# Five edits to the data movement of a convolution-and-token-mixing kernel: x in DRAM by chunks, merged halo copies, channel weights and chunk 2 at other times

## Chip, cores, metric

One core of a Trainium2 chip (trn2). The metric is the device time of one execution in microseconds (us); medians are over executions. The profile is one execution on that core, taken by the hardware profiler.

## The reference, cut to what matters

```python
# x: (8, 4224, 192), weight: (8, 7); w_tok_r, w_tok_i: (4224, 4224); w_theta, w_ch: (192, 192)
w = softmax(weight)                                   # 7 taps for each of 8 heads
x = causal_conv(x, w)                                 # along the sequence, by head
theta = x @ w_theta
zr, zi = x * cos(theta), x * sin(theta)
y = einsum('ts,bsd->btd', w_tok_r, zr) + einsum('ts,bsd->btd', w_tok_i, zi)
u = x + y
out = u + maximum(u @ w_ch, 0.0)
```

The two products over the sequence (4224 by 4224, 1536 columns) are nearly all of the arithmetic. The kernel makes them in seven real products in place of eight, by sums of the weights and of zr and zi.

## The kernel before: what the change and the argument touch

The sequence is cut into 33 chunks of 128 tokens, each of four runs of 32 tokens from the four quarters of the sequence. A chunk is loaded, convolved, rotated (`theta`, `product`, `sums`) and kept in SBUF as the moving operand. Eleven chunks are held at a time. A *step* goes over the chunks held, for two tiles of 128 output tokens; its weights are loaded by GpSimd's queue (`load_w`: 4 loads of w_tok_r, 4 of w_tok_i), transposed by VectorE in 32-blocks (`turn`) and combined (`wsum`). In the *ramp*, the first 110 us, the first eleven chunks come in while the first steps already run.

```python
xs = dram.tile([S, N], F16, name="xs")       # the convolved x, kept in DRAM for the residual
...
class Chunk:
    def __init__(self, k, before=None):
        self.xw = wk.tile([2 * WR, 2, B, D], F16, name="xw", tag="big", bufs=6)
        for a in range(NQ):                           # the four quarters
            h, lo = a // 2, (a % 2) * WR
            t0 = token(k, a)
            hist = self.xw[lo : lo + HALO, h, :, :]
            if before is not None:                    # 16 tokens of the chunk before
                nc.sync.dma_start(
                    out=hist, in_=before.xw[lo + Q : lo + Q + HALO, h, :, :]
                )
            ...
            nc.gpsimd.dma_start(                      # 96 KB of x
                out=self.xw[lo : lo + n, h, :, :],
                in_=x[:, t0 : t0 + n, :].rearrange("b s d -> s b d"),
            )
    def conv(self, j):
        ...
        if j == 1:
            for a in range(NQ):                       # four stores of 96 KB
                t0 = token(self.k, a)
                nc.sync.dma_start(out=xs[t0 : t0 + Q, :], in_=self.x[a * Q : (a + 1) * Q, :])
...
st = wpool.tile([P, 2, NQ, NW * Q], F16, name="st", tag="st", bufs=2)   # in load_w: two buffers
...
steps[0].load_rows()
for m in (1, 2):
    steps[0].load_w(m)      # weights r, then i, of step 0
load_chunk(2)
for m in (1, 2):
    steps[1].load_w(m)      # each needs the buffer that step 0's transposes free
for i in range(NW + 2):     # the ramp: one round a chunk
    ...
    if i + 3 < NW:
        load_chunk(i + 3)
    ...
dve(nc.vector.memset(wch[:, 1:3, :], 0.0))            # at the end of the ramp
for rows, i, part_w in channel_pieces(moe_w_ch):
    nc.gpsimd.dma_start(out=wch[rows, i, :], in_=part_w)
```

The weights' staging tile `st` has two buffers: the r half of step 1 can only be loaded when the r half of step 0 has been transposed, and the i half when the i half has. And GpSimd issues in the order of the program: in the trace of before, chunk 3's load goes out at 20.96 us, behind step 1's weights.

## Time and profile before

| | before |
|---|---|
| time, first three runs | 1445.77, 1449.16, 1449.5 us |
| profiled span | 1446.4 us |
| TensorE busy | 1416.3 us (98%) |
| TensorE busy in the first 110 us | 92.2 us |
| TensorE idle from 110 to 1370 us | 2.9 us |
| granted TensorE clock, mean | 0.998 |

Read it from the last rows up: the middle of the kernel is full, so the time can only change at the two ends, and the ramp is the larger. The lines behind this are in the prediction below.

### The profile page before, as it was taken

What the parts mean: (1) busy time and instruction counts of PE and PEld (TensorE: products, weight loads), DVE (VectorE), ACT (ScalarE), POOL (GpSimd) and SP (SyncE); (2) the same over time, 40 slices, a digit from 0 to 9 for tenths busy, and PEclk for the clock granted to TensorE, in tenths of its full rate; (3) what the DMA queues carried; (4) which work ended last, traced back from release to release, by engine and by line L of the source; (5) the groups of instructions that cost most, each with busy time, mean ns of one, the idle gap of its engine ahead of it and who ended that gap; (6) DMA issues with size and microseconds to landing.
All of it is one profiled execution on the core that took longest, in us unless ns stands there. A gap on an engine that the chain in (4) does not pass through costs nothing.

```text
span 1446.4 us, 23748 instructions
## 1 busy us (share of the span) xinstructions
PE 1416.3 (98%) x9809; PEld 887.9 (61%) x9809; DVE 979.2 (68%) x1051; ACT 315.5 (22%) x379; POOL 435.1 (30%) x655
## 2 busy tenths in 40 slices
PE   7899999999999999999999999999999999999997
PEld 5556666666666666666666666666666666666665
DVE  6893555545548777866666657877777667767686
ACT  5861101111134254000000004435210110010133
POOL 7431211111233232432433342233323123213120
PEclk9999999999999999999999999999999999999999
DMA  9986756465699998998899989999999999998893
GB/s 173 227 178 145 146 103 149 90 149 97 137 231 219 214 250 217 228 254 183 213 256 213 242 143 245 228 188 234 279 216 206 209 204 221 204 203 194 166 222 125
DMA packets 272029, 281.99 MB, mean 195 GB/s; under 512 B 106672, under 2 KB 240176, under 8 KB 271920
## 3 DMA queue, kind: packets, MB, share of 16 engines
q0 software_dynamic: 162464, 92.15, 48.4%
q1 hardware_dynamic: 71824, 178.88, 35.1%
q10 hardware_dynamic: 37632, 9.44, 4.1%
q8 instruction: 77, 1.26, 0.3%
q14 instruction: 32, 0.26, 0.1%
HBM read 245.49 MB, written 108.13 MB: 244 GB/s over the span
## 4 chain that ended last, share of the span: by engine, by line
PE 89%; DVE 4%; DMA 3%; POOL 2%; ACT 1%; issue 1%; SPq 0%; DVEq 0%; ACTq 0%; POOLq 0%
PE y L443 82%; PE v L141 5%; PE pc L210 1%; PE tp L165 1%; POOL st L323 1%; DMA xw<-in_x_dram 1%; DVE z L257 1%; DVE wt L336 1%; DVE pv L408 1%; ACT z L246 1%; DVE z L251 0%; DVE pv L476 0%; DVE wt L348 0%; POOL xw L197 0%; DMA xs<-z 0%
## 5 line engine op out<-in xcount | busy, mean ns | idle before, releaser
L443 PE MATMUL y<-z,wt 128*128 128x384 f16 x7656 | 1283.6, 326 | 10.6 <-DVE pv L408 7.5
L443 PEld LDWEIGHTS <-wt 128*128 128x128 f16 x7656 | 740.8, 98 | 488.6 <-issue 10.6
L408 DVE TENSOR_TENSOR pv<-y,pv 128x768 f32<-128x768 f32 x324 | 308.9, 954 | 323.6 <-PE y L443 282.8
L336 DVE STREAM_TRANSPOSE wt<-st 128x1408 f16<-128x1408 f16 (+7 forms) x224 | 327.8, 1465 | 48.5 <-PE y L443 39.0
L323 POOL DMA_DIRECT2D st<-in_moe_w_tok_r_dram x232 | 132.5, 578 | 466.1 <-DVE wt L336 461.0
L323 POOL DMA_DIRECT2D st<-in_moe_w_tok_i_dram x232 | 132.7, 578 | 404.4 <-DVE wt L336 388.9
L348 DVE TENSOR_TENSOR wt<-wt 128x1408 f16<-128x1408 f16 (+7 forms) x216 | 176.7, 818 | 40.8 <-PE y L443 38.4
L151 ACT ACTIVATE z<-pc 128x768 f16<-128x768 f32 x65 | 53.2, 819 | 387.2 <-PE pc L210 386.9
L151 ACT ACTIVATE ub<-pv 128x768 f16<-128x768 f32 x63 | 50.2, 835 | 333.0 <-DVE pv L408 310.4
L406 ACT ACTIVATE pv<-y 128x768 f32<-128x768 f32 x66 | 54.0, 819 | 282.0 <-PE y L443 282.0
L141 PEld LDWEIGHTS <-uT 128*128 128x128 f16 x1056 | 91.0, 98 | 25.8 <-issue 7.9
L386 POOL TENSOR_TENSOR pv<-pv,xr 128x1536 f32<-128x1536 f32 x24 | 74.5, 3105 | 68.6 <-DVE pv L476 22.1
L197 POOL DMA_DIRECT2D xw<-in_x_dram x132 | 76.4, 585 | 31.0 <-DMA xw<-xw 8.7
L476 DVE SCALAR_TENSOR_TENSOR pv<-v,pv 128x768 f32<-128x768 f32 x66 | 62.9, 954 | 27.5 <-PE v L141 27.1
L257 DVE TENSOR_TENSOR z<-z 128x768 f16<-128x768 f16 x132 | 73.4, 556 | 3.6
L151 ACT ACTIVATE uT<-tp 128x1536 f16<-128x1536 f16 (+1 forms) x48 | 58.2, 1215 | 74.4 <-PE tp L165 74.4
L246 ACT ACTIVATE z<-v,half_pi 128x768 f16<-128x768 f32 x66 | 59.8, 907 | 41.2 <-PE v L141 40.8
L251 DVE TENSOR_TENSOR z<-z 128x1536 f16<-128x1536 f16 x66 | 60.0, 947 | 7.5 <-ACT z L246 7.5
L141 PE MATMUL v<-wth,uT 128*128 128x192 f16 x528 | 55.0, 248 | 4.4 <-ACT z L246 3.0
L141 PE MATMUL v<-wch,uT 128*128 128x192 f16 x528 | 54.2, 246 | 2.1 <-DVE pv L476 1.2
L246 ACT ACTIVATE z<-v 128x768 f16<-128x768 f32 x66 | 53.4, 809 | 0.0
L210 PE MATMUL pc<-xw,bands 96*64 96x192 f16 x528 | 35.8, 258 | 2.6 <-ACT bands L625 1.1
(44 smaller groups left out, 142.4 us busy)
## 6 DMA issues: line engine op xcount, KB each, us to landing
part<-pv SPq DMA_DIRECT2D x79, 768.0 KB, 4.3
pv<-part SPq DMA_DIRECT2D x79, 768.0 KB, 6.1
out_dram<-pv SPq DMA_DIRECT2D x66, 384.0 KB, 4.3
st<-in_moe_w_tok_r_dram POOLq DMA_DIRECT2D x136, 176.0 KB, 5.5
st<-in_moe_w_tok_i_dram POOLq DMA_DIRECT2D x136, 176.0 KB, 5.1
xs<-z SPq DMA_DIRECT2D x132, 96.0 KB, 4.5
xw<-in_x_dram POOLq DMA_DIRECT2D x121, 96.0 KB, 6.1
xr<-xs SPq DMA_DIRECT2D x24, 384.0 KB, 3.7
```

The source lines that it names most:

```text
L141: pe(nc.tensor.matmul(v[:, k, b * D : (b + 1) * D], lhsT=tT[:, 3 * k + b + i, :], rhs=w[:, 2 * b + i, :], start=(i == 0), stop=(i == 1),))
L151: act(nc.scalar.activation(out=out, in_=in_, func=AT.Copy))
L197: nc.gpsimd.dma_start(out=self.xw[lo : lo + n, h, :, :], in_=x[:, t0 : t0 + n, :].rearrange("b s d -> s b d"),)
L246: act(nc.scalar.activation(**args))
L257: dve(nc.vector.tensor_tensor(out=z[:, o, :], in0=z[:, a, :], in1=z[:, b, :], op=ALU.subtract))
L323: pool(nc.gpsimd.dma_start(out=st[a * Q : (a + 1) * Q, 0:nb, :, 0:n] .rearrange("i r bt s -> i (r bt) s"), in_=w[self.tbs[0] * P : (self.t ...
L336: dve(nc.vector.transpose(self.w[name][:, 0 : self.n, :, :], self.st[int(name[1])][:, int(name[0]) - 1, :, 0 : self.n * Q] .rearrange("p b ...
L348: dve(nc.vector.tensor_tensor(out=self.w[name][:, 0 : self.n, :, :], in0=self.w[a][:, 0 : self.n, :, :], in1=self.w[b][:, 0 : self.n, :, : ...
L386: ins = pool(nc.gpsimd.tensor_tensor(out=self.pv[i], in0=self.pv[i], in1=self.xr[i], op=ALU.add))
L408: dve(nc.vector.tensor_tensor(out=o, in0=yv, in1=o, op=ALU.add))
L443: pe(nc.tensor.matmul(y[cn][:, q, 0:BH], lhsT=self.w[wn][:, c, :, :].rearrange("p bt i -> p (bt i)"), rhs=chunks[k].z[:, zn, q * BH : (q + ...
L476: dve(nc.vector.scalar_tensor_tensor(out=ub, in0=channel_mix(self.uT[i][:, 6 * g : 6 * g + 6, :], wch), scalar=0.0, in1=ub, op0=ALU.max, o ...
```

## The change

The intent: fewer DMA issues on SyncE in the ramp (one store of x a chunk in place of four; halo rows of both halves in one copy, so two copies a chunk in place of four), the load of the channel weights taken off the end of the ramp into a quiet step, and x of chunk 2 on GpSimd's queue ahead of the weights of step 0.

```diff
-    xs = dram.tile([S, N], F16, name="xs")
+    xs = dram.tile([NK, P, N], F16, name="xs")
 ...                                                   # Chunk.__init__
+            for lo in (0, WR) if before is not None else ():
+                nc.sync.dma_start(
+                    out=self.xw[lo : lo + HALO, :, :, :],
+                    in_=before.xw[lo + Q : lo + Q + HALO, :, :, :],
+                )
 ...                                                   # the copies of one half each are gone
-                    nc.sync.dma_start(
-                        out=hist, in_=before.xw[lo + Q : lo + Q + HALO, h, :, :]
-                    )
+                    pass
 ...                                                   # conv
-                for a in range(NQ):
-                    t0 = token(self.k, a)
-                    nc.sync.dma_start(
-                        out=xs[t0 : t0 + Q, :], in_=self.x[a * Q : (a + 1) * Q, :]
-                    )
+                nc.sync.dma_start(out=xs[self.k, :, :], in_=self.x)
 ...                                                   # load_x: x read back, four loads for one
-            nc.sync.dma_start(
-                out=self.xr[i], in_=xs[self.tbs[i] * P : (self.tbs[i] + 1) * P, :]
-            )
+            for j in range(NQ):
+                a, k = divmod(NQ * self.tbs[i] + j, NK)
+                nc.sync.dma_start(
+                    out=self.xr[i][j * Q : (j + 1) * Q, :],
+                    in_=xs[k, a * Q : (a + 1) * Q, :],
+                )
 ...                                                   # step_events
+        if t == NU - 2:
+            def load_wch():
+                dve(nc.vector.memset(wch[:, 1:3, :], 0.0))
+                for rows, i, part_w in channel_pieces(moe_w_ch):
+                    pool(nc.gpsimd.dma_start(out=wch[rows, i, :], in_=part_w))
+            found.append((3, load_wch))
 ...
     steps[0].load_rows()
+    load_chunk(2)
     for m in (1, 2):
         steps[0].load_w(m)
-    load_chunk(2)
 ...
-    dve(nc.vector.memset(wch[:, 1:3, :], 0.0))
-    for rows, i, part_w in channel_pieces(moe_w_ch):
-        nc.gpsimd.dma_start(out=wch[rows, i, :], in_=part_w)
```

Cut: the accumulating stores of the last tiles (`add_ahead`), which now go by runs of rows in the new layout.

More of the change, by code (lines that the diff above doesn't have):

```diff
@@ L133, in token, with x_rows @@
         return (a * NK + k) * Q
+    def x_rows(tb):
+        found = []
+        for j in range(NQ):
+            a, k = divmod(NQ * tb + j, NK)
+            if found and found[-1][2] == a:
+                found[-1][1].append(k)
+            else:
+                found.append((j * Q, [k], a))
+        return [
+            (slice(lo, lo + len(ks) * Q), slice(ks[0], ks[-1] + 1), slice(a * Q, (a + 1) * Q))
+            for lo, ks, a in found
+        ]
     def channel_mix(tT, w):
@@ L185, in __init__ @@
                 t0 = token(k, a)
-                hist = self.xw[lo : lo + HALO, h, :, :]
                 if before is not None:
-                    nc.sync.dma_start(
-                        out=hist, in_=before.xw[lo + Q : lo + Q + HALO, h, :, :]
-                    )
+                    pass
                 elif t0 == 0:
-                    nc.vector.memset(hist, 0.0)
+                    nc.vector.memset(self.xw[lo : lo + HALO, h, :, :], 0.0)
                 else:
@@ L378, in load_x @@
             self.xr[i] = wk.tile([P, N], F16, name="xr", tag="xr", bufs=1)
-            nc.sync.dma_start(
-                out=self.xr[i], in_=xs[self.tbs[i] * P : (self.tbs[i] + 1) * P, :]
-            )
+            for j in range(NQ):
+                a, k = divmod(NQ * self.tbs[i] + j, NK)
[3 more added lines that the diff above has]
+                )
         def add_x(self, i):
@@ L393, in add_ahead @@
             tb = self.tbs[i]
-            for cols in (slice(0, HN), slice(HN, N)):
-                pool(nc.gpsimd.dma_start(
-                    out=part[which][tb, :, cols], in_=xs[tb * P : (tb + 1) * P, cols],
-                    accum_op=ALU.add,
-                ))
+            for rows, ks, a in x_rows(tb):
+                for cols in (slice(0, HN), slice(HN, N)):
+                    pool(nc.gpsimd.dma_start(
+                        out=part[which][tb, rows, cols].rearrange("(k i) n -> i k n", i=Q),
+                        in_=xs[ks, a, cols].rearrange("k i n -> i k n"), accum_op=ALU.add,
+                    ))
         def give(self, y, i, h, copies):
```

## The prediction

> **What bounds the kernel now.** I read the page first for the share of each engine, then a table of stretches to see where TensorE is not full, then the waits and the timeline of those stretches, and last the landing times of the single DMAs there.
>
> The first lines of the page:
>
> ```profile
> PE 1416.3 (98%) x9809; PEld 887.9 (61%) x9809; DVE 979.2 (68%) x1051; ACT 315.5 (22%) x379; POOL 435.1 (30%) x655
> ...
> PE   7899999999999999999999999999999999999997
> ```
>
> TensorE is full except in the first slices and the last. The table by stretches (length; then busy us of PE, PEld, DVE, ACT, POOL; granted clock, DMA share, GB/s) gives sizes:
>
> ```profile
> 30.00:40.00 10.00, 6.58 (x56) 4.28 (x55) 8.22 (x15) 7.07 (x9) 4.58 (x8) 0.94 1.30 212
> ...
> 100.00:110.00 10.00, 7.54 (x48) 4.33 (x46) 9.79 (x12) 0.63 (x1) 3.40 (x6) 1.00 0.59 78
> 110.00:400.00 290.00, 290.00 (x1786) 174.64 (x1785) 145.51 (x126) 38.31 (x48) 58.58 (x103) 1.00 0.61 128
> ...
> 1030.00:1370.00 340.00, 340.00 (x2275) 216.78 (x2274) 241.14 (x237) 37.84 (x48) 97.22 (x122) 1.00 0.95 204
> 1370.00:1447.00 77.00, 67.00 (x547) 46.14 (x544) 54.34 (x67) 25.70 (x33) 9.34 (x17) 0.99 0.67 173
> ```
>
> From 110 to 1370 us TensorE misses 2.9 us in all (0 in the two long stretches shown; 0.73, 0.73 and 1.41 in the three between them). The idle 30.1 us (1446.4 less 1416.3) lie at the two ends: about 17 us in the first 110 us (the ramp, in which the first 11 chunks of x are convolved, rotated and multiplied) and 10 us in the last 77. The start-to-start time of two large matmuls in the trace has a median of 163 ns[...]. In the ramp the idle time is less than what is lost: 33 dummy matmuls and a granted clock of 0.89 to 0.94 between 30 and 50 us are in it too. Counting the matmuls that the ramp needs by their spacing in the trace (258 large ones at 163 ns, 176 at 82 ns, 132 transposes at 56 ns, 22 convolutions of about 0.5 us, 2.5 us for the bands) gives about 77 of 110 us. So some 33 us, 2.3% of the span, is the most that any repair of the ramp alone could earn.
>
> The waits of TensorE in the ramp (total us, times, longest), and the rows of the timeline (start, duration) that the change touches:
>
> ```profile
> PE y L443 <- DVE pv L408: 5.1, 5, 2.5
> ...
> PE pc L210 <- DMA xw<-in_x_dram: 0.9, 1, 0.9
> ```
>
> ```profile
> 12.36 2.29 POOL L197 DMA_DIRECT2D xw<-in_x_dram  x4
> ...
> 16.41 2.29 POOL L323 DMA_DIRECT2D st<-in_moe_w_tok_r_dram  x4 [1.77 <-DVE wt L336]
> ...
> 20.96 4.57 POOL L197 DMA_DIRECT2D xw<-in_x_dram  x8
> ...
> 27.70 0.52 PE L210 MATMUL pc<-xw,bands 96*64 96x192 f16 x7 [0.88 <-DMA xw<-in_x_dram]
> ...
> 103.52 0.22 DVE L699 MEMSET wch<- 128x192 uint32 x1
> 103.66 0.90 DVE L408 TENSOR_TENSOR pv<-y,pv 128x768 f32<-128x768 f32 x1
> ...
> 104.61 10.57 PE L443 MATMUL y<-z,wt 128*128 128x384 f16 x64 [2.46 <-DVE pv L408]
> ```
>
> The load at 12.36 is chunk 2. The one wait of TensorE for x, at 27.70, is for chunk 3, whose fourth piece was issued at 22.67 and landed at 27.66; it was not chunk 2, whose pieces landed from 15.7 to 18.9 while its convolution ran at 20.53 in program order, after dummies.
>
> [...]
>
> **The change part by part.** *One store of x a chunk.* 132 stores become 33. One takes SyncE 0.42 us to issue (tile view of xs in the ramp), so 99 x 0.42 = 42 us of issue go, 1.3 us a chunk. VectorE later overwrites the x that the store reads, which must wait for it. But the group of those subtractions (L257) has 3.6 us of idle time in the whole run and none of it is put down to a DMA. On the path: 0.
>
> *Halo copies.* 120 become 60, at 0.54 us: 32 us of SyncE go. A copy must still wait for the last of the loads of the chunk before; only the copies ahead of the last one shrink. TensorE has no wait for a halo copy in its list. On the path: 0, perhaps 0.3 us gained through less traffic at 20 to 28 us.
>
> *x read back.* 24 loads of 384 KB become 96 of 96 KB: 72 x 0.42 = 30 us of SyncE added, and the last of four is issued 1.3 us later. GpSimd's additions waited 2.3 us in all for these loads and VectorE 1.3 us for one addition, in a stretch where TensorE lost 0.7 us. On the path: 0, at worst 1. The accumulating stores go from 18 to 20: of the nine late tiles only one spans two quarters of the sequence. GpSimd is busy 97 of 340 us there: 0.
>
> *Channel weights.* The memset sits on VectorE at 103.52, straight ahead of the addition that TensorE waits for; VectorE has no gap from 85.6 us on. It delays that addition by 103.66 - 103.52 = 0.14 us (operations overlap a little). Gain 0.14, and with it may go up to 1 us of GpSimd waiting that nobody waits for. In its new place, around 3/7 of the sixteenth step, VectorE is half idle: 0.
>
> *Chunk 2 sooner.* On GpSimd's queue its four issues, 2.29 us, go from 12.36 to 7.77, and the token weights of step 0 go back by 2.3 us. In the trace these landed at 11.7 to 13.0 and 13.2 to 14.7, and VectorE took them at 15.35 and 16.36. Moved by 2.3 us, the first half lands at up to 15.4 and the second at up to 17.0, so the transposes at 15.35 and 16.36 slip by 0.1 to 0.6 us. Their end frees the buffer for the issue at 16.41; from there GpSimd issues without a break to the load of chunk 3, which may be 0.5 us later. But that DMA queue was moving data without pause from 20 to 28 us, and chunk 2's bytes are now out of the way earlier, so its landing should move by less: -0.5 to +0.5, taken as 0. What chunk 2 itself gains is invisible, for its convolution did not wait.
>
> Sum on the path: 0.14 sure, about 0.3 from lighter traffic, 0 to 1 against it. I take a gain of 0.5 us from the page's kernel. The three plain runs (1445.77, 1449.16, 1449.5) average 1448.1; less the gain that is 1447.6, and I say 1447.8.
>
> **Rivals.** (a) The early order matters more: after 30 us ScalarE and VectorE pass the chunks on with little slack (ScalarE 9.3 to 9.9 of each 10 us from 40 to 60), so a start of chunk 3 that moves early or late shifts the whole ramp[...]. For it: the chain of waits runs through the issue at 16.41 and the landing at 27.66. Against: the chunk that moves is not the one waited for. It would make 2 to 4 us either way: 1444 to 1451. (b) The SyncE queue is the hidden brake of the ramp: between 19 and 33 us it issues almost without a pause, and a third less of it frees halo copies and stores by 1 to 2 us a chunk. For it: copies landed 4 to 6 us after issue. Against: TensorE waited for no halo copy, VectorE for no store. If true, 3 to 6 us faster, 1442 to 1445. (c) Four loads in the place of one hold up SyncE's in-order queue in the middle, and partial sums come late. For it: SyncE waited 73.7 us for GpSimd at this load. Against: there are only 24 such tiles, in a stretch where TensorE hardly waits. One late addition in four would cost 24/4 x 1.3 = 8 us: 1456.
>
> **Range and chances.** The runs of before spread over 3.7 us, more than the effect. The range takes that spread, (a) whole and the near end of (b): 1444.6 to 1450.8. Faster by 2% means under 1420; even (b) is far from it, and only the whole 33 us of the ramp would do: 0.01. Slower by 2% needs 29 us, several times (c): 0.01.
>
> **What would show it.** Right: TensorE still busy about 1416 us and idle about 30; 110 to 1370 us unchanged; the wait for chunk 3 near 27 us still there within 1 us; the wait at the end of the ramp about 0.15 us shorter with no memset ahead of it; SyncE's issues for xs, halo and x read back at 33, 60 and 96. Wrong: if the first step of full rate comes more than 2 us sooner or later than 104.6, (a) or (b) holds; if waits of large matmuls for VectorE between 520 and 1370 us grow, (c).

Its sum: 0.14 us sure, about 0.3 from lighter traffic (estimate, for which no trace is named), 0 to 1 against it, taken together as a gain of 0.5. That the middle is full rests on TensorE's 2.9 us of idle time from 110 to 1370 us; that its matmuls could not follow one another faster than every 163 ns was not shown.

## The result, and the profile after

| | before | after |
|---|---|---|
| median (range; executions) | 1448.92 (1445.77 to 1449.5; 4) | 1451.8 (1451.25 to 1452.16; 4) |
| ratio, after over before | | 1.0024, 95% interval 1.0007 to 1.0041 |
| profiled span | 1446.4 | 1449.5 |
| TensorE busy in the first 110 us | 92.2 | 88.95 |

A ratio here is the mean time of one kernel's fast runs over that of the other's of the same rounds, so it is not quite the ratio of the medians that are quoted. The change is some 3 us slower, where a gain of about 0.5 was predicted, and 1451.8 lies 1.0 us above the end of the predicted range.

First the page of the kernel after:

```profile
PE 1416.0 (98%) x9809; PEld 887.7 (61%) x9809; DVE 976.6 (67%) x1051; ACT 315.4 (22%) x379; POOL 437.7 (30%) x657
...
PE   7789999999999999999999999999999999999997
```

TensorE's work is the same (1416.0 against 1416.3 us), so the 3.1 us are idle time, and the second and third slices are at 7 and 8 where they were at 8 and 9. The stretches of the kernel after (length; busy us of PE, PEld, DVE, ACT, POOL; clock, DMA share, GB/s) say the same:

```profile
20.00:30.00 10.00, 7.55 (x60) 4.67 (x57) 8.78 (x15) 5.10 (x7) 7.80 (x14) 0.83 0.96 163
30.00:40.00 10.00, 5.95 (x58) 4.12 (x59) 6.99 (x12) 8.01 (x10) 5.89 (x11) 1.00 1.35 217
...
110.00:400.00 290.00, 290.00 (x1786) 174.66 (x1785) 147.87 (x129) 38.12 (x47) 59.25 (x105) 1.00 0.62 127
1030.00:1370.00 340.00, 340.00 (x2271) 216.53 (x2270) 241.36 (x236) 37.84 (x48) 97.44 (x120) 1.00 0.98 204
```

From 110 to 1370 us TensorE is idle for 2.9 us, as before: so the four loads of x read back, the new place of the channel weights and the accumulating stores cost nothing on the path. From 20 to 30 us it executes 60 matmuls; in the kernel before the same stretch is

```profile
20.00:30.00 10.00, 8.25 (x86) 5.57 (x85) 9.56 (x14) 6.94 (x10) 7.84 (x14) 1.00 1.36 206
```

26 more, at a full clock, and with the DMA engines at 206 GB/s in place of 163. The loss begins there. The waits of TensorE in the first 115 us of the kernel after (total, times, longest):

```profile
PE y L459 <- DVE pv L424: 6.0, 6, 2.3
...
PE v L155 <- DVE uT L163: 1.9, 2, 1.8
PE pc L226 <- DMA xw<-in_x_dram: 1.7, 1, 1.7
```

The wait of the convolution for x of chunk 3 has gone from 0.9 to 1.7 us, and a wait of 1.8 us for a copy by VectorE is new. Where do they come from? The timeline of the kernel after (start, duration, engine, operation; in brackets the idle time before it and what ended it):

```profile
7.77 2.32 POOL L213 DMA_DIRECT2D xw<-in_x_dram  x4
...
13.31 2.42 SPq L198 DMA_DIRECT2D xw<-xw  x4
13.86 1.72 POOL L335 DMA_DIRECT2D st<-in_moe_w_tok_i_dram  x3 [0.92 <-DMA xw<-in_x_dram]
...
20.45 0.45 DVE L348 STREAM_TRANSPOSE wt<-st 128x256 f16<-128x256 f16 x1 [4.11 <-DMA st<-in_moe_w_tok_i_dram]
...
22.20 2.29 POOL L335 DMA_DIRECT2D st<-in_moe_w_tok_i_dram  x4 [3.60 <-DVE wt L348]
...
23.16 0.83 PE L155 MATMUL v<-wth,uT 128*128 128x192 f16 x8 [1.77 <-DVE uT L163]
...
24.48 5.70 POOL L213 DMA_DIRECT2D xw<-in_x_dram  x10
...
31.28 0.52 PE L226 MATMUL pc<-xw,bands 96*64 96x192 f16 x7 [1.70 <-DMA xw<-in_x_dram]
```

Read it as one chain, from the top:

1. Chunk 2 is issued at 7.77 (12.36 before). The i half of step 0's weights follows behind it; three of its four issues also wait 0.92 us.
2. The landing records put the four pieces of that half at 14.9, 18.0, 18.9 and 20.3 us (before: 13.2 to 14.7).
3. VectorE's transpose of it stands idle for 4.11 us and starts at 20.45 (before: 16.36). In VectorE's order the copy of chunk 1's transpose stands behind it and is late as well (22.15 against 19.71): the 1.77 us wait of TensorE at 23.16.
4. That transpose and the next (it ends at 21.91) free the staging buffer: step 1's i half goes out at 22.20 (before: 18.68), and chunk 3 behind it at 24.48 (before: 20.96).
5. Chunk 3 lands 3.6 us later (last piece 31.2 against 27.66), and TensorE waits for it.

Between steps 3 and 4 the delay shrinks from 4.10 to 3.52 us. In the kernel before, the second transpose of the i half ended at 17.80, but GpSimd came to the issue that waits for it only at 18.68:

```profile
16.36 0.44 DVE L336 STREAM_TRANSPOSE wt<-st 128x256 f16<-128x256 f16 x1
...
17.36 0.44 DVE L336 STREAM_TRANSPOSE wt<-st 128x256 f16<-128x256 f16 x1
...
18.68 2.29 POOL L323 DMA_DIRECT2D st<-in_moe_w_tok_i_dram  x4
```

In the kernel after, the issue follows the end of that transpose by 0.3 us (21.91 and 22.20). So before had about 0.6 us to spare, and only what a slip has beyond that reaches chunk 3.

From here the two traces are parallel. Against the first trace of the kernel before, the evacuation of chunk 3's convolution is 3.58 us later, VectorE's transpose at 56.4 us is 3.09 later, and everything after 107 us is 2.94 later. (The step from 3.58 to 3.09 lies where the trace of before has a window at half clock, explained below.) The 0.15 us between the last two is the memset, which no longer stands ahead of this addition:

```profile
106.54 0.95 DVE L424 TENSOR_TENSOR pv<-y,pv 128x768 f32<-128x768 f32 x1
```

### The profile page after: what moved, and what is told of

Same layout as the page of the kernel before. It is cut to its first block, busy times and chain, and to the rows that moved or that the text cites. A ratio compares the mean times of both kernels' runs of the same rounds, so it can differ in the third digit from the quotient of the medians.

```text
span 1449.5 us, 23566 instructions
## 1 busy us (share of the span) xinstructions
PE 1416.0 (98%) x9809; PEld 887.7 (61%) x9809; DVE 976.6 (67%) x1051; ACT 315.4 (22%) x379; POOL 437.7 (30%) x657
## 2 busy tenths in 40 slices
DMA packets 269707, 281.97 MB, mean 195 GB/s; under 512 B 105312, under 2 KB 238816, under 8 KB 269600
## 4 chain that ended last, share of the span: by engine, by line
PE 90%; DVE 4%; DMA 2%; ACT 2%; POOL 1%; issue 1%; DVEq 0%; SPq 0%; POOLq 0%; ACTq 0%
PE y L459 82%; PE v L155 5%; PE tp L179 1%; PE pc L226 1%; DMA xw<-in_x_dram 1%; ACT z L258 1%; DVE pv L424 1%; DVE z L263 1%; DMA xw<-xw 1%; DVE z L269 1%; ACT uT L165 1%; DVE pv L492 0%; POOL xw L213 0%; DVE wt L360 0%; DVE wt L348 0%
```

## The experiments

The question is which of the edits makes step 0's weights land so late. The expectations name theories by letters. *Theory O*: the new order alone does it; 2.3 us of issues ahead of step 0's weights. *Theory Q*: SyncE's queue does it. In the kernel after, the reads of x for the first tile stand early in SyncE's queue (at 19.02, 22.58 and 30.76 us; before, the first such read is at 82.6), and they wait there for the stores to land (7.1 us in two waits, the longest 4.0), with the halo copies behind them. *Theory B*: the *merged halo copies* or the *single store* crowd the DMA engines. *Theory D* is the late landing read above, whatever makes it; *theory C* is that executions differ only in how many windows at half clock they meet.

**How small differences were told apart.** Every kernel was timed, but the intervals of a ratio are about 0.0013 either way, some 2 us, not much less than the effect. So each kernel's trace was also laid beside the first trace of the kernel before, operation by operation, and three shifts were read: VectorE's third transpose (16.36 us before), the evacuation of chunk 3's convolution (28.25 us), and the end of the ramp (VectorE's additions after 165 us). All shifts below are against that one trace; + is later. It has a half-clock window of its own at 38.87 us: against kb_before, whose ramp has none, every figure of the last column is 1.17 larger (4.11 for after).

| kernel | median us | ratio to before, 95% interval | third transpose | chunk 3 evacuated | end of ramp |
|---|---|---|---|---|---|
| after | 1451.8 | 1.0024 (1.0007 to 1.0041) | +4.10 | +3.58 | +2.94 |
| k0_after (the same again) | 1452.5 | 1.0015 (1.0001 to 1.0029) | +3.08 | +2.77 | +3.57 |
| kb_before (before again) | 1449.59 | 1.0009 (0.9995 to 1.0023) | +0.05 | -0.25 | -1.17 |
| k1_order | 1449.17 | 1.0003 (0.9987 to 1.0019) | +1.03 | -0.50 | -1.41 |
| k3_halo | 1450.32 | 1.0 (0.9988 to 1.0013) | +0.03 | +1.61 * | +3.58 * |
| k4_layout | 1449.99 | 1.0009 (0.9997 to 1.0021) | +0.04 | +2.88 * | +4.63 * |
| k2_noorder | 1451.6 | 1.001 (0.9998 to 1.0022) | +0.44 | +2.45 * | +3.89 * |
| k6_all_minus_halo | 1450.96 | 0.9997 (0.9981 to 1.0014) | +1.92 | +2.42 * | +4.62 * |
| **k1b_order_halo** | 1451.66 | 1.0019 (1.0007 to 1.0031) | +4.27 | +3.00 | +4.71 (* 1.68 of it) |
| k14_order_halo_split | 1449.96 | 1.0004 (0.9993 to 1.0016) | +0.36 | +0.08 | +1.36 (* 1.68 of it) |
| k5_wch | 1449.94 | 0.9999 (0.9987 to 1.0011) | +0.06 | +0.25 | +0.12 |
| k10_before_c3 | 1450.21 | 1.0007 (0.9994 to 1.002) | +0.03 | -0.64 | +1.78 (* 1.68 of it) |
| k12_order_c3_wch | 1450.54 | 1.0008 (0.9996 to 1.002) | +1.10 | -0.64 | -0.75 |
| k15_after_c3 | 1449.14 | 1.0001 (0.9988 to 1.0014) | +2.47 | -0.97 | -0.67 |
| k7_held | 1456.24 | 1.0053 (1.0033 to 1.0073) | +4.27 | +3.33 | +3.62 |
| k9_held_c3 | 1453.12 | 1.0031 (1.0004 to 1.0058) | +2.90 | -0.68 | +0.56 |

(*) A window at half clock sits in these figures. What it explains of them, and what it does not, comes first.

**The windows at half clock.** In 13 of the 17 kept traces TensorE is granted half its clock in some windows of 3.41 us of the ramp. The clock records of the traces of before and after have two values, 1.0 and 0.5, and in the ramp lengths that are whole multiples of 3.413 us: 23.893 us (7 times) at full clock and 3.413 at half in the kernel before, 10.240 (3 times) and 3.413 in the kernel after. Three stretches of the first trace of the kernel before, then the last of them in kb_before, which is the same program (the number after POOL's is the clock):

```profile
32.05:35.46 3.41, 1.90 (x16) 1.05 (x14) 2.61 (x4) 3.41 (x5) 2.96 (x6) 1.00 1.25 199
35.46:38.87 3.41, 1.79 (x16) 0.81 (x15) 3.26 (x7) 1.61 (x3) 1.15 (x2) 1.00 1.30 221
38.87:42.28 3.41, 3.41 (x22) 2.12 (x21) 3.38 (x6) 2.06 (x3) 1.91 (x4) 0.50 0.64 97
```

```profile
38.87:42.28 3.41, 2.83 (x30) 2.06 (x29) 3.41 (x6) 2.89 (x5) 2.17 (x4) 1.00 0.94 135
```

A window with 1.79 us of busy TensorE (52%) was followed by one at half clock, with 22 matmuls where kb_before ran 30 in less busy time. The window before these in the first trace, from 32.05 us, was busy for 1.90 us (56%) and was followed by a full clock. Busy time alone does not decide it: windows that were 41% busy (k4_layout, at 105.37 us) and 44% (k9_held_c3, at 103.27) were followed by a full clock too. What brings the half clock was not shown. The half-clock window starts at 38.87 us in the first trace of before and at 24.32 in that of after, and kb_before, the program of before, has none in the ramp; so they are counted here as chance between executions. By the two figures of the trace such a window would cost 3.41 x 0.5 = 1.7 us where TensorE is the limit (an estimate); the shift measured across one at 105 to 112 us was 1.68 (k1b_order_halo, k3_halo, k10_before_c3). The two traces of before differ by 1.17 us at the end of the ramp; how much of the spread of that kernel, from 1445.77 to 1454.9 in all rounds, such windows make was not shown. They make single traces at the end of the ramp poor witnesses. The first two shifts are better ones. Where half-clock windows lie before 32 us, the evacuation is starred, but the clock is the smaller part of those figures. In k2_noorder, k3_halo, k4_layout and k6_all_minus_halo TensorE first waited for a DMA, in a window that it filled to 12 to 33%, and the half clock followed; it lengthened the seven matmuls before the evacuation from 0.52 to 0.82 or 0.85 us. The rest of 1.6 to 2.9 us is the wait for the DMA. Not starred are after and k7_held, whose window at 24.3 and 24.6 us is followed by a wait of TensorE for chunk 3 (1.7 and 1.5 us), so that it cost nothing there, and k14_order_halo_split, whose window from 8.86 to 19.1 us slowed matmuls (the eight of a convolution took 0.85 us at 14.01 and 17.14, 0.52 at 21.33). In k14_order_halo_split, k2_noorder and k6_all_minus_halo a full-clock window lies before that, from 5.3 to 5.5 us on, and the first store of x went out 1.1 us sooner than in the other traces (11.79 against 12.8 to 12.9).

### One part of the change at a time

**k1_order**: the kernel before, with chunk 2 moved ahead alone.

```diff
     steps[0].load_rows()
+    load_chunk(2)
     for m in (1, 2):
         steps[0].load_w(m)
-    load_chunk(2)
```

> The kernel before with nothing changed but the place of chunk 2's load on GpSimd's queue, ahead of the token weights of step 0. Theory O (order: the weights of step 0 now wait behind chunk 2 in GpSimd's one ring, so VectorE's third transpose of the ramp, at 16.36 us before and 20.45 us after, is late and everything behind it too): the third transpose at 19 to 20.5 us and the whole span 2 to 3.5 us longer than before. Theory B (burst: the one store of x and the merged halo copies crowd the DMA engines just when the second half of these weights is under way): the third transpose at no later than 17.5 us and the span within 1 us of before.

The i half landed at 15.0 to 17.3 us and the transpose slipped by 1.03 us, no more:

```profile
17.38 0.45 DVE L336 STREAM_TRANSPOSE wt<-st 128x256 f16<-128x256 f16 x1 [1.28 <-DMA st<-in_moe_w_tok_i_dram]
...
21.40 6.92 POOL L197 DMA_DIRECT2D xw<-in_x_dram  x12
```

Chunk 3 was issued 0.44 us later (21.40 against 20.96) and evacuated 0.50 sooner; the ratio is 1.0003. (Of the slip of 1.03, 0.6 was to spare.) Theory O falls: alone, the new order does nearly what the prediction said of it.

**k2_noorder**: the kernel after, with chunk 2 put back.

```diff
     steps[0].load_rows()
-    load_chunk(2)
     for m in (1, 2):
         steps[0].load_w(m)
+    load_chunk(2)
```

> The kernel after with chunk 2's load put back behind the token weights of step 0; store, halo copies and channel weights stay changed. Theory O: the third transpose back at 16.4 us within 0.5, the span at or 0.2 us below before. Theory B: the third transpose still 1 us or more late, the span 1 us or more above before. Theory Q (queue: the reads of x for one tile now sit among the first entries of SyncE's in-order queue and hold up halo copies behind them): the third transpose in time, but conv of chunks 3 to 5 late, span 1 to 3 us above before.

The transpose was at +0.44 us: without the order the late weights are gone. But chunk 3 was late by another way, the one that theory Q names: its halo copies stood in SyncE's queue behind a read of x that waited for a store, went out only at 23.09 and landed at 28.57, and TensorE waited 2.7 us for them and then 0.9 us for x. The half clock from 29.24 us came after that. The median of 1451.6 has an interval that includes 1, so the time is inconclusive.

**k3_halo** and **k4_layout**: the kernel before with the merged halo copies alone, and with the new layout of x (one store, four loads, accumulating stores by runs) alone.

```diff
+            for lo in (0, WR) if before is not None else ():        # k3_halo
+                nc.sync.dma_start(
+                    out=self.xw[lo : lo + HALO, :, :, :],
+                    in_=before.xw[lo + Q : lo + Q + HALO, :, :, :],
+                )
 ...
-                for a in range(NQ):                                 # k4_layout
-                    t0 = token(self.k, a)
-                    nc.sync.dma_start(
-                        out=xs[t0 : t0 + Q, :], in_=self.x[a * Q : (a + 1) * Q, :]
-                    )
+                nc.sync.dma_start(out=xs[self.k, :, :], in_=self.x)
```

> The kernel before with the merged halo copies alone. Theory O and Q: within 0.5 us of before. Theory B: part of the loss, 0.5 to 1.5 us above before.

> The kernel before with the layout of x in DRAM alone: one store a chunk, four loads for a tile, the accumulating copies by groups of rows. Theory O: within 0.5 us of before. Theory B: 0.5 to 1.5 us above. Theory Q: 1 to 3 us above, with the convolution of chunk 3 or 4 late although its x has landed, and SyncE seen waiting for stores of x ahead of halo copies.

Neither moved the transpose (+0.03 and +0.04), and neither interval excludes 1. So no part alone makes step 0's weights as late as in the kernel after, and two together are to be tried. But chunk 3 was late in both traces. In k4_layout a read of x waited in SyncE's queue for a store up to 23.18, and the halo copies of chunk 3 behind it, the last of which landed at 30.14; its x had landed by 27.40:

```profile
23.18 0.32 SPq L391 DMA_DIRECT2D xr<-xs  x1
23.59 2.41 SPq L202 DMA_DIRECT2D xw<-xw  x4
...
28.53 0.24 PE L224 MATMUL pc<-xw,bands 96*64 96x192 f16 x1 [1.46 <-DMA xw<-xw]
...
30.28 0.82 PE L224 MATMUL pc<-xw,bands 96*64 96x192 f16 x7 [1.50 <-DMA xw<-xw]
```

This is what the expectation gave as the sign of theory Q. In k3_halo TensorE waited 1.9 us for x of chunk 3, issued 0.8 us later than in before. These are executions of 1452.1 and 1452.35 us, above the medians of their kernels; whether the others did the same is not on record, and the ratios (1.0009 and 1.0) show no clear loss.

**k5_wch**: the channel weights moved alone.

```diff
+            found.append((3, load_wch))       # in the step t == NU - 2
 ...
-    dve(nc.vector.memset(wch[:, 1:3, :], 0.0))
```

> The kernel before with the channel weights alone in their new place. By the prediction 0.14 us: in the trace the addition after the two subtractions at the end of the ramp comes 0.1 to 0.2 us sooner against the steps just before it; the timed runs within 0.5 us of before, which the spread hides.

This trace's half-clock window lies within 0.3 us of where the first trace of before has it. It is 0.27 us late up to the end of the ramp and 0.12 from there: the step is 0.15 us.

### Is it SyncE's queue?

**k0_after** is the kernel after once more, on another chip, as the companion of the next three.

> The kernel after once more, beside before on one chip. What is to be told apart: whether its first trace was typical. Theory D (delay by DMA): the second half of step 0's weights lands at 17.9 us or later again, the third transpose is 3 us or more late and chunk 3's convolution 3 us late in this trace too, and the timed runs are close together 2 to 3 us above before. Theory C (clock: what differs between executions of all these kernels is how many 3.4 us windows at half TensorE clock fall into the ramp, and the change only meets another number of them): the third transpose less than 2 us late in this trace, and the timed runs spread over 3 us or more.

It shows the loss again, in the trace and in the time (1.0015, interval above 1).

**k7_held**: the kernel after, with each read of x made to wait for VectorE's latest work, so that it can't stand early in SyncE's queue.

```diff
-                nc.sync.dma_start(
+                ld = nc.sync.dma_start(
                     out=self.xr[i][j * Q : (j + 1) * Q, :],
                     in_=xs[k, a * Q : (a + 1) * Q, :],
                 )
+                tc.add_manual_dep(ld.ins, last["dve"].ins.name, SYNC, reason="pace")
```

> The kernel after with each read of x held until VectorE reaches the place where the program asks for it, so that none can sit early on SyncE's queue. Theory Q (these reads block halo copies and stores behind them): 1.5 to 3 us faster than after. Theory D without Q: the third transpose is still late by 3 us and the span within 1 us of after.

The reads left the ramp, and the ramp stayed: +4.27, +3.33, +3.62. Theory Q falls for the ramp of the kernel after: there the halo copies of chunk 3 are issued at 14.57 and 15.20, ahead of the reads. (In k4_layout and k2_noorder they stand behind them, and wait.) The edit does harm of its own: at 608 us reads that now come late hold up an addition, and TensorE waits

```profile
PE y L460 <- DVE pv L425: 2.4, 1, 2.4
```

which with a half-clock window behind it makes 4.2 us, and another 6 follow between 1235 and 1280 us, where GpSimd waits 16.2 us for such a read.

**k6_all_minus_halo**: the kernel after, with the four separate halo copies of before.

```diff
-            for lo in (0, WR) if before is not None else ():
-                nc.sync.dma_start(
-                    out=self.xw[lo : lo + HALO, :, :, :],
-                    in_=before.xw[lo + Q : lo + Q + HALO, :, :, :],
-                )
 ...
+                    nc.sync.dma_start(
+                        out=hist, in_=before.xw[lo + Q : lo + Q + HALO, h, :, :]
+                    )
```

> The kernel after with four separate halo copies a chunk. If the merged copies of chunks 2 and 3, which start back to back at 13.3 to 15.2 us, take the DMA engines from the second half of step 0's weights (theory B): these land 2 us or more earlier than in after, as they did with the order alone (17.3 us), and the span is 1.5 to 3 us shorter than after. Otherwise (store or order): no more than 0.5 us.

Ratio 0.9997 beside 1.0015 for k0_after in the same rounds; the i half landed at 17.0 to 18.2 and the transpose was at +1.92. Without the merged copies about half of the slip is gone, and the timed runs are those of before, though the two intervals overlap. The trace, of one of the slower executions (1452.06 us), does not show the gain at chunk 3: the last piece of x landed at 29.75, 7.5 us after the first was issued, TensorE waited 2.3 us for it, and the evacuation was 2.42 us late. So the merged copies are not shown to be needed for the loss in the kernel after; that they are enough with the order is shown next.

**k9_held_c3**: k7_held, with chunk 3 loaded ahead of step 1's weights.

```diff
     for m in (1, 2):
         steps[0].load_w(m)
+    load_chunk(3)
     for m in (1, 2):
         steps[1].load_w(m)
```

> The kernel after with the reads held and chunk 3 loaded before the weights of step 1, in the time in which GpSimd waits for a weight buffer. If the wait of TensorE for chunk 3 carries the loss (theories D and Q), conv of chunk 3 starts at 26 to 28 us in place of 31.8, and the span is 3 to 4 us below after, so at or 1 us below before. If the loss is the clock's alone (theory C), no more than 1 us below after.

The transpose stayed late (+2.90) but chunk 3 came 0.68 us sooner than before, and the ramp lost only 0.56. The 4.7 us near 608 us are the harm of holding the reads.

### Two parts together

**kb_before** is the kernel before again, run as the others are: the noise of the method.

> The kernel before once more, for a second trace of it. If the half-clock windows of TensorE are placed by chance and not by the kernel (theory C for the spread between executions), this trace has another set of them than the first (one, at 38.9 us), and its ramp ends at another time by 1 us or more although every DMA and VectorE step up to 27 us is within 0.5 us of the first; its timed runs spread over 3 us again.

Ratio 1.0009 for the same program. A ratio of 1.001 in the table is therefore no finding. Its trace has no half-clock window in the ramp and ends it 1.17 us sooner than the first.

**k1b_order_halo**: the kernel before, with chunk 2 ahead and the merged halo copies; nothing else.

```diff
     steps[0].load_rows()
+    load_chunk(2)
     for m in (1, 2):
         steps[0].load_w(m)
-    load_chunk(2)
 ...                                                   # and, in Chunk.__init__,
+            for lo in (0, WR) if before is not None else ():
+                nc.sync.dma_start(
+                    out=self.xw[lo : lo + HALO, :, :, :],
+                    in_=before.xw[lo + Q : lo + Q + HALO, :, :, :],
+                )
```

> The kernel before with the early chunk 2 and the merged halo copies, and no other part. Each alone cost nothing clear. If the loss comes from the two together (the halo copies of chunk 2 and 3 fall on the second half of step 0's weights only when chunk 2 is early): that half lands at 18 us or later, the third transpose at 19 us or later, chunk 3's convolution 2 us late, span 1.5 to 3 us above before. If the single store of x is needed as well: the third transpose at no more than 18 us and the span within 1 us of before.

This is a loss of the same size: ratio 1.0019 with an interval above 1, and the chain of the kernel after link by link. Its timeline:

```profile
20.62 0.45 DVE L338 STREAM_TRANSPOSE wt<-st 128x256 f16<-128x256 f16 x1 [4.13 <-DMA st<-in_moe_w_tok_i_dram]
...
24.63 6.89 POOL L199 DMA_DIRECT2D xw<-in_x_dram  x12
...
29.54 0.24 PE L212 MATMUL pc<-xw,bands 96*64 96x192 f16 x1 [1.23 <-DMA xw<-in_x_dram]
...
30.70 0.52 PE L212 MATMUL pc<-xw,bands 96*64 96x192 f16 x7 [0.92 <-DMA xw<-in_x_dram]
```

Up to 31.25 us, where chunk 3 is evacuated 3.00 us late, its trace has no half-clock window behind the first matmuls, so the clock is not the cause. Neither is the single store or the layout needed for this loss.

**k10_before_c3** and **k12_order_c3_wch** tried for a faster kernel: before with chunk 3 ahead of step 1's weights, and the same with chunk 2 ahead and the channel weights moved. The edit is the `load_chunk(3)` line of k9_held_c3.

> The kernel before with chunk 3, and not chunk 2, loaded sooner: ahead of the weights of step 1, in GpSimd's idle 1.8 us at 14.6 us. Chunk 3 is what TensorE waited for. Its convolution no longer waits for x; 1 to 2 us faster than before where the clock is the same, so 1446.5 to 1448.5 us.

> The kernel before with chunk 2 early, chunk 3 ahead of the weights of step 1 and the channel weights in their new place; store and halo copies as before. The candidate for a version that beats both: 1 to 2.5 us faster than before, and 3 to 5 us faster than after. If the second half of step 0's weights is pushed back by chunk 2 as in after, no gain over the run with chunk 3 alone.

Both miss. In k10_before_c3 TensorE's wait for chunk 3, 0.9 us in before, is gone, and chunk 3 is evacuated 0.64 us sooner; but chunk 4's evacuation is 0.77 us later, and up to a half-clock window at 105 us the ramp is at +0.10, with an earlier such window (36.83) much where the trace of before has its own (38.87). What was gained was given back at once; what took it was not followed up.

### Why the merged copies?

A merged copy moves the bytes of two (96 KB for two of 48). What differs is when they go and in what pieces. Merged, all of chunk 2's halo goes out behind the first store of x (13.35 and 13.97 us in k1b_order_halo); unmerged, half of it goes at 9.2 to 9.8. And the trace's DMA records show pieces of 6144 bytes, with medians of mostly 240 to 420 ns in stretches of 2 us, in place of 3072 bytes and about 130; step 0's weights come in 2048 pieces of 128 bytes, 32 ns each.

**k14_order_halo_split** tells these apart. Each copy spans both halves, as the merged ones do, but is cut in two by batch.

```diff
+            for lo in (0, WR) if before is not None else ():
+                for bs in (slice(0, GB), slice(GB, B)):
+                    nc.sync.dma_start(
+                        out=self.xw[lo : lo + HALO, :, bs, :],
+                        in_=before.xw[lo + Q : lo + Q + HALO, :, bs, :],
+                    )
```

> The kernel before with the early chunk 2 and halo copies that span both halves but are cut in two by batch: four a chunk, of the old size, yet each waiting for the loads of both halves as the merged ones do. If the merged copies hurt by their larger packets, the second half of step 0's weights lands by 17.3 us and the third transpose comes by 17.5 us, as with the order alone. If they hurt because a copy that needs both halves cannot be issued before the store of x of chunk 0 and so falls at 13 to 16 us, on those weights: the third transpose at 19 us or later and the span 2 to 3 us above before.

All four copies of chunk 2 go out behind the first store, from 12.26 to 14.22 us, with the bytes of k1b_order_halo; their pieces are of 1536 bytes, about 70 ns each. The i half landed at 15.5 to 16.6:

```profile
16.72 0.45 DVE L339 STREAM_TRANSPOSE wt<-st 128x256 f16<-128x256 f16 x1 [0.54 <-DMA st<-in_moe_w_tok_i_dram]
```

The weights' pieces of 128 bytes, by the microsecond in which they started, show the crowding itself:

| pieces of step 0's weights in | 14 to 15 | 15 to 16 | 16 to 17 | 17 to 18 | after 18 us |
|---|---|---|---|---|---|
| k1_order (halo in 3072 bytes) | 341 | 511 | 107 | 0 | 0 |
| k14_order_halo_split (1536 bytes) | 566 | 449 | 0 | 0 | 0 |
| k1b_order_halo (6144 bytes) | 301 | 405 | 410 | 124 | 39 |
| after (6144 bytes, one store) | 252 | 92 | 378 | 276 | 22 |

From 14.5 to 15.5 us, 16 pieces of the merged copies and 265 of the weights started in k1b_order_halo; in k14_order_halo_split, 67 pieces of the split copies, as many bytes within 5%, and 522 of the weights. In the kernel after it were 12 pieces of the merged copies, 85 of the single store (3072 bytes) and 15 of the weights, so that gap is in the main the store's. Why fewer of the weights' pieces start beside larger ones was not shown: the trace doesn't name the engine of a piece, so these are counts over all engines.

The size of the pieces fits best, then, and neither the bytes nor the place behind the store. That k14_order_halo_split runs about 1 us ahead is not the difference: from the issue of the last of the four loads of the i half to its landing it took 2.6 us there, 3.0 in k1_order and 5.7 in k1b_order_halo. (A small part lies before the issue: in k1b_order_halo GpSimd waited 0.72 us for a landing of x before it issued these loads, and in the kernel after 0.92; in k14_order_halo_split it did not wait.) But the merged copies are also two of 96 KB for four of 48 KB; one copy of 96 KB in small pieces was not tried. It is one trace for each of these kernels, but the landings of the last of the i half fall apart over all traces with chunk 2 early: 18.7 to 20.5 us in the six with merged copies, 16.6 to 18.2 in the four without. The timed ratios, 1.0004 for the split copies and 1.0019 for the merged, agree with it, but their intervals still touch.

**k15_after_c3**: the kernel after with `load_chunk(3)` ahead of step 1's weights. If TensorE's wait for chunk 3 carries the loss, this repairs it though the weights stay late.

> The kernel after with nothing changed but chunk 3 loaded ahead of the weights of step 1. The third transpose stays late by 3 us or more. If the wait of TensorE for chunk 3 is what carries that delay into the span: its convolution at 27.5 to 28.5 us in place of 31 to 31.8, the ramp's lag behind the first trace of before under 1 us where after had 2.9 to 3.6, and 2 to 3 us faster than after, at before or 1 us above. If not: within 0.7 us of after.

The transpose was still late (+2.47, less than the 3 us expected); the convolution of chunk 3 was not, nor did it wait:

```profile
18.82 0.45 DVE L348 STREAM_TRANSPOSE wt<-st 128x256 f16<-128x256 f16 x1 [1.58 <-DMA st<-in_moe_w_tok_i_dram]
...
26.72 0.52 PE L226 MATMUL pc<-xw,bands 96*64 96x192 f16 x8
```

Its ramp ends at -0.67 us, which is 0.50 later than that of kb_before (neither has a half-clock window), where the kernel after is 4.11 later; its ratio is 1.0001. The last link of the chain is shown. No kernel tried is clearly faster than before.

## Why the prediction was right or wrong, by its own steps

- **What bounds the kernel: right.** TensorE's busy time is unchanged and 110 to 1370 us as full as before; the whole difference arises in the ramp.
- **One store of x a chunk, x read back, accumulating stores: right within the noise.** The middle lost nothing, so rival (c) is refuted (k4_layout 1.0009, kb_before 1.0009). The early reads of x in SyncE's queue were not foreseen. k7_held shows that they are not what cost the time in the kernel after; in k4_layout and k2_noorder they made TensorE wait 3.0 and 2.7 us for halo copies.
- **Channel weights: right.** 0.14 predicted; 0.15 in k5_wch, k2_noorder and the kernel after.
- **Halo copies, "On the path 0, perhaps 0.3 us gained through less traffic": wrong in sign.** There is no less traffic, for the bytes are the same: 60 copies of 96 KB for 120 of 48 KB, and 281.97 MB in all against 281.99. There are larger pieces (6144 bytes in place of 3072), and with chunk 2 early the weights of step 0 landed late beside them (k1b_order_halo).
- **Chunk 2 sooner: the step that failed.** It said that the second half of step 0's weights lands "at up to 17.0", so that "the transposes at 15.35 and 16.36 slip by 0.1 to 0.6 us", and that chunk 3's landing moves by "-0.5 to +0.5, taken as 0". Measured: 20.3, 4.1 us and +3.6. For the order alone (k1_order) the working was nearly right: 17.3, 1.0 and, at the evacuation, -0.5. One reading of the lines was wrong here: the transpose at 16.36 does not free the buffer for the issue at 16.41. That issue is of the r half, which the two transposes at 15.35 free; the transposes at 16.36 and 17.36 are of the i half and free it for the issue at 18.68, with 0.6 us to spare. What failed was to cost each part by itself against the trace of before. The shift by 2.3 us put these weights into the very microseconds in which the first store and chunk 2's halo go out, and another part of the change had made those pieces larger. In before the last of these weights landed at 14.7, ahead of the store (15.6) and of the copies issued at 13.3 and 13.9 (16.3 and 18.1).
- **Rival (a) had the right chain, but not the whole cause.** It laid the loss to the order alone, which k1_order refutes; the merged copies had to come with it. It named the chain (buffer freed at 16.41, chunk 3 landing at 27.66) and its size, 2 to 4 us. "Against: the chunk that moves is not the one waited for" was the wrong reason to set it aside: the moved chunk delays the weights, and these the chunk that is waited for. Rival (b), a gain from less of SyncE's queue, found no support: with 60 copies and 33 stores in place of 120 and 132 no trace showed a gain.
- **The range** ended at 1450.8. The gain assumed (0.5) and the loss found (2.9 by the medians) differ by 3.4 us, more than half of its width. The spread of before, 1445.77 to 1454.9 us in all rounds, was rightly named as larger than the effect.

What stays open: the share of the single store and of the reads of x in the kernel after (k6_all_minus_halo still slips by 1.92 us against 1.03 in k1_order, and has chunk 3 late in its one trace; so have k2_noorder and k4_layout); and the tail of these loads, 22 and 39 pieces after 18 us, which sets the landing and which the trace can't assign to an engine.

## What to carry to other kernels

When a load is moved, look up which transfers are in flight in the microseconds that it moves into, and with what sizes of pieces, in the kernel as it will be with all parts of the change, not as it was. Follow a buffer's release through the order of a queue to the load behind it: in the kernel after, chunk 2, which nobody waited for, went ahead of step 0's weights, and beside the merged copies and the one store chunk 3 landed 3.6 us later; TensorE waited 1.7 us for it, 0.9 in before. Merging the halo copies saved 60 issues, which brought no gain, and made pieces of 6144 bytes; with chunk 2 early, the last of the weights, which come in pieces of 128 bytes on another queue, landed at 20.5 us (k1b_order_halo) in place of 17.3 (k1_order), and at 16.6 beside pieces of 1536 bytes (k14_order_halo_split).
